# RetNet attention feeding a gated MLP on one core: the new state's product moved ahead of the state's product with the queries

## The chip, the cores and the metric

The kernel runs on one NeuronCore of a Trainium2 chip. The metric is the device time of one execution in microseconds (us), and the time of a kernel is the median over several executions.

## The reference

Two blocks stand one behind the other. The first is RetNet's parallel attention, with no softmax: for 8 batches, 8 heads, 576 positions and a head width of 64,

```python
scores = q @ k.T / sqrt(64)
gamma  = 1 - 2 ** (-5 - arange(8))                 # one decay for each head
Dmat   = where(i >= j, gamma ** (i - j), 0)        # i: query position, j: key position
ret    = (scores * Dmat) @ v
```

The heads' results are laid side by side as rows of `x`, 4608 tokens by 512. The second block is an MLP with a "serf" activation:

```python
h = x @ w_in                                       # 512 -> 2048
g = h * erf(softplus(h))
out = g @ w_out                                    # 2048 -> 512
```

All is in float32.

## The kernel before

**Attention in pieces.** The 4608 tokens are cut into 36 pieces of 128 tokens (`pieces`). Each pair of batches gives nine: four whole pieces of the first batch, four of the second, and a last one that holds the two batches' remaining 64 tokens each. Since the decay is a power, earlier tokens need not be multiplied again: their keys and values are summed into a *state* of 64 by 64 for each head, which is carried from piece to piece (`kept`). Decay factors are folded into the values (`gk`, on GpSimd in `weigh_values`), into the outputs (`gq`) and into the state (`gp`).

**Three stages for a piece.** `transposes` brings queries and keys to the layout that TensorE wants. For the first pieces TensorE does it (L332) with copies on ScalarE, for the later ones VectorE (L326), out of tiles `raw_qs` and `raw_ks` that SP's queue loads in 32-wide squares (L131). `scores` multiplies keys with queries (L347, 8 matmuls, tile `s`), and VectorE masks them into `sT` (L99). `outputs` is the stage that the change touches. It has up to three groups of 8 matmuls into two PSUM tiles of one bank each, `o[0]` and `o[1]`:

- the *outputs' products* (L365): values by masked scores, `o<-sT,raw_v`; contraction over 128 rows, 64 columns out, 128 moving columns
- the *state's products with the queries* (L376), `o<-qT,state`, only where the piece does not begin its batch: contraction over 64 rows, 64 columns out, 128 moving columns (64 in the nine-piece group's last piece, where two states are used)
- the *new state's product* (L388), `o<-raw_v,raw_k`, in whole pieces only: contraction over 128 rows, 64 columns out, 64 moving columns. It goes into the upper half of `o[0]`'s bank, which the code calls `kv`.

Of the 36 pieces, 8 begin a batch (no L376), 24 have all three groups, and 4 are the shared last ones (no L388).

VectorE then takes the results out, through the helper `tt` (L99): `scaled(1)` moves `o[1]`, times `gq`, into `x`; `sums` adds the old state to `kv`, and GpSimd multiplies by `gp` into `state` or `last` (L427; in a batch's first piece VectorE does that directly); `scaled(0)` moves `o[0]`. The four PSUM banks of the pool `ps_at` are shared in turn by `pt`, `s` and `o`.

**The MLP.** It works on chunks of 512 tokens and four slices of the hidden width. `First.product` (L496) is `x @ w_in`, `Second.product` (L604) is `g @ w_out`; both replace eight block products by seven with sums made on VectorE (a Strassen-Winograd form, `sums`, `operands_x`). In the first slice the first two chunks take a plain form (L550), and the last block of all has a form of its own (L668). Their matmuls are 128 by 128 with 256 moving columns. Weights are loaded in pieces and rounded by a chain of operations (`rounding`, L254 to L275) on ScalarE, VectorE and GpSimd.

**What sets the order.** The program's order is written by hand, and each engine works through its own instructions in that order. The stages stand in one list,

```python
    for i in range(len(pieces)):
        stages += [(transposes, i + 1), (outputs, i), (scores, i + 1)]
```

and `attend` issues the next one between steps of the MLP, so that a stage of attention alternates with a block product until the pieces are used up. A string at the start (`"alkakakawk..."`) orders the first chunk. SP's queue issues nearly all transfers in program order: `load(i + 2, "q")` at the end of `transposes(i)`, `load(i + 3, "kv")` at the end of `outputs(i)`, and stores of `x` and of partial outputs between them. Waits between engines are set by the framework from the tiles that instructions read and write.

Of the kernel before, what the change touches and what calls it, by code (L numbers as in the profile page):

```python
# [21 lines left out]
NP = H // 2  # L22
# [32 lines left out]
def kernel(  # L55
# [10 lines left out]
    nc = tc.nc  # L66
# [31 lines left out]
    def tt(out, in0, in1, op):  # L98
        nc.vector.tensor_tensor(out=out, in0=in0, in1=in1, op=op)  # L99

    def flat(ap):
        return ap.rearrange("p h d -> p (h d)")

    heads = [slice(e * D, (e + 1) * D) for e in range(2)]
# [45 lines left out]
    def load(i, names="qkv"):  # L150
        if i < len(pieces):
            t = loaded.setdefault(i, {})
            for name in names:
                src = {"q": q, "k": k, "v": v}[name]
                if name == "q" and i < SQUARES:
                    t["q"] = load_rows(i, "q", q, 2)
                elif name == "q":
                    t["qs"] = load_squares(i, "q", q)
                    if i >= SQUARES_K:
                        t["ks"] = load_squares(i, "k", k)  # L160
                elif name == "v" or i < SQUARES_K or len(pieces[i]) == 1:
                    t[name] = load_rows(i, name, src, 4)
# [137 lines left out]
    def x_tile():  # L300
        return xpool.tile([P, n_dc + 3, TCH], FP32, tag="x", name="x")
# [4 lines left out]
    def weigh_values(i):  # L306


        if i < len(pieces) and i not in weighed:
            weighed.add(i)  # L310
            t = (loaded.get(i) or live[i])["v"]
            by = gk if len(pieces[i]) == 1 else gk2
            nc.gpsimd.tensor_tensor(out=t, in0=t, in1=by.unsqueeze(2).to_broadcast([P, H, D]), op=ALU.mult)
# [40 lines left out]
    def outputs(i):  # L354
        segments = pieces[i]
        t = live.pop(i)
        seen = [(kept[b], r0, n) for b, s0, n, r0 in segments if s0 > 0]

        b, s0, n, _ = segments[0]
        o = [ps_at.tile([P, NP, P], FP32, tag="at", name=f"o{j}") for j in range(2)]
        for p in range(NP):
            for e in range(2):
                nc.tensor.matmul(  # L365
                    o[p % 2][heads[(e + p) % 2], p // 2, :],
                    lhsT=t["v"][:, 2 * p + e, :],
                    rhs=t["sT"][:, e, p, :],
                    start=(p < 2),
                    stop=(not seen and p >= NP - 2),  # L370
                    skip_group_check=True,
                )
        for state, r0, m in seen:
            for p in range(NP):
                for e in range(2):
                    nc.tensor.matmul(  # L376
                        o[p % 2][heads[(e + p) % 2], p // 2, r0 : r0 + m],
                        lhsT=state[heads[e], p, :],
                        rhs=t["qT"][heads[e], p, r0 : r0 + m],
                        start=False,  # L380
                        stop=(p >= NP - 2),
                        skip_group_check=True,
                    )
        if n == P:
            kv = flat(o[0])[:, 2 * P :].rearrange("p (a d) -> p a d", a=NP)
            for p in range(NP):
                for e in range(2):
                    nc.tensor.matmul(  # L388
                        kv[heads[e], p, :],
                        lhsT=t["k"][:, 2 * p + e, :],  # L390
                        rhs=t["v"][:, 2 * p + e, :],
                        start=False,
                        stop=(p == NP - 1),
                        skip_group_check=True,
                    )
        c, at = i // PC, i % PC * P
        if (0, c) not in x:
            x[0, c] = x_tile()

        def scaled(j):  # L400
            to = x[0, c][:, j:NP:2, at : at + P]
            if c < n_ch - 1:
                by = (gq if n == P else gq2)[:, j::2, :].unsqueeze(2).to_broadcast([P, 2, P // n, n])
                dst, got = (y.rearrange("p a (m i) -> p a m i", i=n) for y in (to, o[j][:, :2]))
                tt(dst, got, by, ALU.mult)
                return

            for r0 in range(0, P, n):
                dst = to[:, :, r0 : r0 + n].rearrange("p h (r a) -> p h a r", r=SQ)
                got, by = (  # L410
                    y.rearrange("p h (a r) -> p h a r", r=SQ)
                    for y in (o[j][:, :2, r0 : r0 + n], (gq if n == P else gq2)[:, j::2, :])
                )
                tt(dst, got, by, ALU.mult)

        scaled(1)
        if n == P:
            sums = kv
            if s0 > 0:
                sums = att.tile([P, NP, D], FP32, tag="sums", name="sums")  # L420
                tt(sums, kv, kept[b], ALU.add)

            if b % 2 == 0 and s0 + P + D == S:
                new = att.tile([P, NP, D], FP32, tag="last", name="last", bufs=1)
            else:
                new = att.tile([P, NP, D], FP32, tag="state", name="state")
            (nc.gpsimd if s0 > 0 else nc.vector).tensor_tensor(out=new, in0=sums, in1=gp, op=ALU.mult)  # L427
            kept[b] = new
        scaled(0)
        load(i + 3, "kv")  # L430
        if i + 1 >= SQUARES:
            weigh_values(i + 1)

    stages = [(transposes, 0), (scores, 0)]
    for i in range(len(pieces)):
        stages += [(transposes, i + 1), (outputs, i), (scores, i + 1)]
        if i in (PC + 1, 2 * PC - 1):
            stages[-3:-1] = stages[-2], stages[-3]
# [3 lines left out]
    def before_chunk(c):  # L442

        return stages.index((outputs, c * PC)) if c < n_ch else len(stages)

    def after_chunk(c):

        return stages.index((outputs, (c + 1) * PC - 1)) + 1
# [415 lines left out]
```

## Time and profile before

| | |
|---|---|
| median of 6 runs | 1027.73 us (1026.16 to 1028.47) |
| the profiled execution, device time | 1027.82 us |
| its span, first to last instruction | 1026.0 us |
| TensorE (PE) busy | 1018.2 us, 99% |
| VectorE (DVE) busy | 668.0 us, 65% |
| ScalarE (ACT) busy | 390.4 us, 38% |
| GpSimd (POOL) busy | 123.6 us, 12% |
| attention, first to last outputs' product | 11.0 to 315 us |
| granted TensorE clock | 1.00 |

In a row of the profile, "L376" is the line of the kernel, PE a matmul and PEld the load of its stationary operand, `o<-qT,state` the tile written and the tiles read. A form such as `64*64` names the part of the array that the instruction uses, rows by columns. A float32 matmul stands as two records, so a group of 8 shows as x16. In timelines the first column is the start in us, the second how long the row's instructions took together, and brackets hold idle time of the engine just ahead and what ended it.

### The profile page before, as it was taken

The numbers are of one execution on the slowest core, as the hardware profiler recorded it, in microseconds if no ns is written. First come the engines' busy times: TensorE is split into PE (matmuls) and PEld (weight loads), VectorE is DVE, ScalarE is ACT, GpSimd is POOL, SyncE is SP. The second block draws the span as 40 slices with busy tenths as digits, with TensorE's granted clock in tenths as the row PEclk, the third lists the DMA queues.
The fourth block names the chain that finished last, engine by engine and source line by source line (L and its number), as shares of the span: only waits on it lengthen the run. The fifth ranks groups of instructions, "written<-read, shape, count | busy, mean of one in ns | idle before, by whom it ended". The sixth has DMA issues, their size and how long they took to land.

```text
span 1026.0 us, 15958 instructions
## 1 busy us (share of the span) xinstructions
PE 1018.2 (99%) x6348; PEld 876.4 (85%) x6348; DVE 668.0 (65%) x1062; ACT 390.4 (38%) x481; POOL 123.6 (12%) x122
## 2 busy tenths in 40 slices
PE   9999999999999999999999999999999999999998
PEld 8787888888788888888888888888888888888887
DVE  3769777877876666656666666666567655555555
ACT  2354134233234444433443344444443333333332
POOL 2133122122311110010001001000100000000000
PEclk9999999999999999999999999999999999999999
DMA  9997989979984344544445344444433334444433
GB/s 198 201 246 166 235 190 228 251 152 247 233 180 168 129 144 144 167 162 160 154 147 174 123 144 154 167 152 144 144 124 124 123 128 128 131 135 131 127 88 118
DMA packets 146986, 165.76 MB, mean 162 GB/s; under 512 B 97376, under 2 KB 121568, under 8 KB 138848
## 3 DMA queue, kind: packets, MB, share of 16 engines
q1 hardware_dynamic: 144832, 163.57, 56.8%
q10 hardware_dynamic: 2080, 1.18, 0.5%
q8 instruction: 50, 0.82, 0.4%
q14 instruction: 24, 0.20, 0.1%
HBM read 117.52 MB, written 47.19 MB: 161 GB/s over the span
## 4 chain that ended last, share of the span: by engine, by line
PE 82%; DMA 10%; DVE 3%; SPq 3%; issue 1%; POOL 1%; ACT 0%; ACTq 0%; DVEq 0%; POOLq 0%
PE a L604 22%; PE a L496 21%; PE g L604 11%; PE g L496 11%; PE e L496 5%; PE e L604 5%; DMA raw_qs<-in_q_dram 4%; DMA raw_v<-in_v_dram 4%; PE o L365 2%; SPq L131 2%; PE s L347 2%; DMA raw_k<-in_k_dram 1%; SPq L147 1%; PE o L388 1%; PE o L376 1%
## 5 line engine op out<-in xcount | busy, mean ns | idle before, releaser
L496 PE MATMUL a<-x,wa 128*128 128x256 f32 x1088 | 258.3, 380 | 0.0
L496 PEld LDWEIGHTS a<-x,wa 128*128 128x128 f32 x1088 | 205.7, 190 | 28.5
L604 PE MATMUL a<-wb,s 128*128 128x256 f32 x840 | 200.0, 381 | 0.0
L604 PEld LDWEIGHTS a<-wb,s 128*128 128x128 f32 x840 | 158.4, 190 | 22.9 <-ACT o L618 0.7
L99 DVE TENSOR_TENSOR t<-g,t 128x512 f32<-128x512 f32 x68 | 46.9, 690 | 150.7 <-ACT t L526 113.1
L496 PE MATMUL g<-x,wa 128*128 128x256 f32 x544 | 129.2, 380 | 0.0
L496 PEld LDWEIGHTS g<-x,wa 128*128 128x128 f32 x544 | 102.8, 190 | 14.4
L99 DVE TENSOR_TENSOR o<-a,o 128x512 f32<-128x512 f32 x104 | 71.4, 686 | 46.5 <-PE a L604 46.5
L521 ACT COPY t<-a 128x512 f32<-128x512 f32 x34 | 19.9, 586 | 188.3 <-PE a L496 188.3
L99 DVE TENSOR_TENSOR t<-t,s 128x1024 f32<-128x1024 f32 x72 | 88.9, 1274 | 0.0
L565 ACT ACTIVATE s<-t 128x1024 f32<-128x1024 f32 x72 | 72.1, 1049 | 28.5 <-DVE t L99 28.4
L274 POOL TENSOR_TENSOR wraw<-wraw 128x512 f32<-128x512 f32 x28 | 29.5, 1052 | 438.4 <-DVE wraw L272 183.2
L99 DVE TENSOR_TENSOR x<-x 128x512 f32<-128x512 f32 x115 | 75.8, 692 | 1.2
L532 ACT COPY t<-a 128x512 f32<-128x512 f32 x34 | 19.9, 586 | 144.3 <-PE a L496 144.3
L569 ACT ACTIVATE s<-s 128x1024 f32<-128x1024 f32 x72 | 72.1, 1048 | 0.4
L604 PE MATMUL g<-wb,s 128*128 128x256 f32 x280 | 66.7, 381 | 0.3 <-DVE t L99 0.3
L604 PE MATMUL e<-wb,t 128*128 128x256 f32 x280 | 66.6, 380 | 0.0
L604 PE MATMUL a<-wb,t 128*128 128x256 f32 x280 | 66.6, 380 | 0.0
L604 PE MATMUL g<-wb,t 128*128 128x256 f32 x280 | 66.3, 380 | 0.0
L99 DVE TENSOR_TENSOR sT<-s,cst 128x512 f32<-128x512 f32 x72 | 46.1, 681 | 29.2 <-PE s L347 29.2
L496 PE MATMUL e<-x,wa 128*128 128x256 f32 x272 | 64.8, 381 | 0.0
L99 DVE TENSOR_TENSOR o<-g,o 128x512 f32<-128x512 f32 x70 | 47.9, 684 | 21.5 <-ACT o L618 18.8
(86 smaller groups left out, 1248.8 us busy)
## 6 DMA issues: line engine op xcount, KB each, us to landing
od<-o SPq DMA_DIRECT2D x54, 512.0 KB, 3.3
x<-xd SPq DMA_DIRECT2D x27, 1024.0 KB, 4.8
o<-od SPq DMA_DIRECT2D x27, 1024.0 KB, 5.1
raw_qs<-in_q_dram SPq DMA_DIRECT2D x96, 112.0 KB, 4.6
raw_ks<-in_k_dram SPq DMA_DIRECT2D x84, 112.0 KB, 4.2
xd<-x SPq DMA_DIRECT2D x9, 1024.0 KB, 5.2
raw_v<-in_v_dram SPq DMA_DIRECT2D x64, 128.0 KB, 4.6
wraw<-in_moe_w_in_dram SPq DMA_DIRECT2D x32, 256.0 KB, 5.9
```

Of the source, the lines that this page charges most:

```text
L99: nc.vector.tensor_tensor(out=out, in0=in0, in1=in1, op=op)
L131: nc.sync.dma_start(out=t[part * SQ : (part + 1) * SQ, :, at : at + m - SQ], in_=tokens[:, :, d0 : d0 + m - SQ])
L147: queue.dma_start(out=t[r0 : r0 + n, e::2, :], in_=heads.rearrange("h p d -> p h d"))
L274: engine.tensor_tensor(out=r_f, in0=high_f, in1=r_f, op=ALU.mult)
L347: nc.tensor.matmul(ps[e][:, p, :], lhsT=t["kT"][heads[e], p, :], rhs=t["qT"][heads[e], p, :], start=True, stop=True)
L365: nc.tensor.matmul(o[p % 2][heads[(e + p) % 2], p // 2, :], lhsT=t["v"][:, 2 * p + e, :], rhs=t["sT"][:, e, p, :], start=(p < 2), stop=(no ...
L496: nc.tensor.matmul(acc[:, j * TH : (j + 1) * TH], lhsT=weights["wa", self.g][:, a, d, j * P : (j + 1) * P], rhs=x[self.g, self.c][a][:, d, :],
L521: nc.scalar.copy(out=self.t1[:, 1], in_=self.a)
L532: nc.scalar.copy(out=self.t2[:, 0], in_=self.a)
L565: nc.scalar.activation(self.s[:, j], t, AF.Softplus)
L569: nc.scalar.activation(self.s[:, j], self.s[:, j], AF.Erf)
L604: nc.tensor.matmul(acc[:, tp, :], lhsT=left[:, j * TH + tp * P : j * TH + (tp + 1) * P], rhs=weights["wb", self.g][:, b, j, :], start=(sta ...
```

## The change

The new state's product stands directly behind the outputs' products, and the state's products with the queries come last. On VectorE, `sums` (or the state itself, in a batch's first piece) is issued ahead of `scaled(1)`, which now directly precedes `scaled(0)`. Nothing is added or removed; in the built program ACT's and SP's instructions stand in the same order as before, and POOL's too.

```diff
-        for state, r0, m in seen:
-            for p in range(NP):
-                for e in range(2):
-                    nc.tensor.matmul(
-                        o[p % 2][heads[(e + p) % 2], p // 2, r0 : r0 + m],
-                        lhsT=state[heads[e], p, :],
-                        rhs=t["qT"][heads[e], p, r0 : r0 + m],
-                        start=False,
-                        stop=(p >= NP - 2),
-                        skip_group_check=True,
-                    )
         if n == P:
             kv = flat(o[0])[:, 2 * P :].rearrange("p (a d) -> p a d", a=NP)
             for p in range(NP):
...
+        for state, r0, m in seen:
+            for p in range(NP):
+                for e in range(2):
+                    nc.tensor.matmul(
+                        o[p % 2][heads[(e + p) % 2], p // 2, r0 : r0 + m],
+                        lhsT=state[heads[e], p, :],
+                        rhs=t["qT"][heads[e], p, r0 : r0 + m],
+                        start=False,
+                        stop=(p >= NP - 2),
+                        skip_group_check=True,
+                    )
         c, at = i // PC, i % PC * P
...
-        scaled(1)
         if n == P:
             sums = kv
...
             (nc.gpsimd if s0 > 0 else nc.vector).tensor_tensor(out=new, in0=sums, in1=gp, op=ALU.mult)
             kept[b] = new
+        scaled(1)
         scaled(0)
```

## The prediction

> **What bounds the kernel now.** I read the page first, for who is busy:
>
> ```profile
> span 1026.0 us, 15958 instructions
> PE 1018.2 (99%) x6348; PEld 876.4 (85%) x6348; DVE 668.0 (65%) x1062; ACT 390.4 (38%) x481; POOL 123.6 (12%) x122
> ...
> PEclk9999999999999999999999999999999999999999
> DMA  9997989979984344544445344444433334444433
> ```
>
> PE has no hole to speak of at full clock, and the DMA engines are near full for the first third, while attention runs (to 315 us), and half idle after it. So time comes off only where PE issues less, or waits less. Next the list of PE's waits, to see what there is to lose or win:
>
> ```profile
> PE pt_q L332 <- DMA raw_q<-in_q_dram: 0.7, 1, 0.7
> PE s L347 <- DVE kT L326: 0.7, 1, 0.7
> PE pt_k L332 <- DMA raw_k<-in_k_dram: 0.4, 1, 0.4
> PE s L347 <- DVE qT L326: 0.4, 1, 0.4
> PE g L604 <- DVE t L99: 0.3, 1, 0.3
> ```
>
> No matmul of the changed stage is in it, and in the same list for the loads only the outputs' products wait for a mask (`sT`, 1.3 us in 4 waits): PE never waits for `state`. An earlier state is thus worth nothing by itself. What can matter is the order on PE, so I read the timeline of one stage with all three groups (106 us) and one that begins a batch (115 us):
>
> ```profile
> 106.12 0.85 PEld L365 LDWEIGHTS o<-sT,raw_v 128*64 128x64 f32 x16 [0.33 <-issue]
> ...
> 107.15 0.43 PEld L376 LDWEIGHTS o<-qT,state 64*64 64x64 f32 x16 [0.17 <-issue]
> ...
> 107.75 0.55 PEld L388 LDWEIGHTS o<-raw_v,raw_k 128*64 128x64 f32 x16 [0.17 <-issue]
> ...
> 108.36 1.59 PEld L604 LDWEIGHTS g<-wb,t 128*128 128x128 f32 x8
> ...
> 115.03 0.85 PEld L365 LDWEIGHTS o<-sT,raw_v 128*64 128x64 f32 x16 [0.33 <-issue]
> ...
> 115.84 0.60 PEld L388 LDWEIGHTS o<-raw_v,raw_k 128*64 128x64 f32 x16
> 116.52 0.51 PEld L496 LDWEIGHTS a<-x,wa 128*128 128x128 f32 x3
> ```
>
> Wherever the form changes (128\*64, 64\*64, 128\*128), the loads pause. Where outputs are followed by the new state's product, both 128\*64, there is no pause. That order occurs 8 times already, and the change makes it the rule. Last the chain of waits, for what could take a gain back:
>
> ```profile
> 37.06 0.42 DVE state L427
> ...
> 42.58 1.09 PE o L365 x14
> ...
> 249.56 6.07 DMA wraw<-in_moe_w_out_dram
> ...
> 260.75 4.75 DMA raw_qs<-in_q_dram
> ...
> 272.64 1.16 PE s L347 x16
> ```
>
> From 158 to 272 us this chain holds transfers, SP and DVE but no PE: PE reaches 272 us only 0.7 us too early. A faster PE will find these loads in its way.
>
> **The change on PE.** Times between the starts of successive groups' loads, in ns. Before, in a stage with all three: outputs 1024, state 598, new state 615, together 2237 (equal within 1 ns in 19 of the 24; the other five contain waits). In the 8 batch beginnings: outputs 819, new state 670, together 1489. After the change a stage is that 1489 plus a state group. Its 598 was measured from a change of form to the next, which is what it has again: the last moving width sets the pause (172 ns behind a width of 128, 68 behind 64, each over two different pairs of forms). So 1489 + 598 = 2087, and 2237 − 2087 = 0.150 us a stage, 24 × 0.150 = 3.6 us if all is kept. If instead the pause belonged to the pair of forms, the new state would take 774 and the state 498: 819 + 774 + 498 = 2091, or 3.5 us. Nothing hangs on that. Bounds on the two boundaries not seen (new state to state; a state of width 128 to the MLP): the nearest rows are those, so I take 0.15 with both ends near.
>
> A rule speaks against this: the Trainium skill, "TensorE: Matmul & The Clock Gate", Part 3, says that a load overlaps running matmuls only if they use other rows of the array. Outputs and new state both use all 128 rows, so by it the boundary would cost its 205 ns again and the whole gain would be near nothing. The trace shows otherwise: at 115.84 us the loads run on, 35 ns ahead of the end of the last output's load. I go with the trace. The other rule, in "TensorEngine Tiling (Array Packing)", Tiling Modes, is that a change of mode drains the array; one of three changes goes, and with the 175 ns of drain on the first page (Single matmul latency) that is an estimate of 4.2 us. The row's 0.150 is net of the longer first group behind it and is used.
>
> **The change on the other engines.** DVE: the same three operations in another order. `sums` does not get free behind the new state's product: it reads `o[0]`, and in the built program it waits for the sixth of the eight state products, the last one into that tile. At the stage of 97 us PE's last product ended at 99.60, DVE began `x` at 98.98, `sums` at 99.64, `x` at 99.97, and was free for the next at 100.30. After: the stage ends 0.15 earlier, the sixth product 0.11 before that (two of eight in 0.43), so `sums` at 99.31, `x` at 99.64 and 99.97, free at 100.30. No change on DVE; the `sums` wait holds up only these two. In a batch's first piece `scaled(1)` used to run beside the new state's product and now stands behind the state operation: DVE is free 0.33 later (starts of 37.06 and 37.40) if it had been waiting there. It was in 3 of 8 (12.1, 36.6, 116.2 us). Of these 36.6 is on the chain, as DVE then works without a gap to the mask that outputs wait for at 42.58: +0.3 us there. The one at 116 is covered: masks end 2.1 us ahead of the outputs around it.
>
> POOL: `state` at most 0.2 us earlier; nobody waits for it. ACT, SP: same order; SP's loads of k and v wait for buffers that come free up to 0.6 us earlier. The new state's product is read for 0.6 us earlier, which needs `raw_k` that was issued three stages before.
>
> **What is kept.** PE's gain lasts until the next moment that others set. Stage by stage:
> - 16, 20, 25 us: lost, since PE then waits for raw_q at 33.9 us.
> - 42, 53, 58 us: +0.45, less 0.3 from DVE, but at 81.8 and 88.3 us PE waits for DVE (0.4 and 0.1), whose chain goes back to weight rounding and loads: about 0.
> - 87.8 to 211.9 us, 11 stages: 1.65. PE waits nowhere, and SP issues each piece's queries when DVE has freed their buffer, so loads follow PE to about 222 us.
> - 220.8, 249.6, 258.8, 267.7 us: up to 0.6, lost in the waits at 252 and 272 us, if transfers stay where they are.
> - 289, 298, 307 us: 0.45, kept; behind them PE alone runs to the end.
>
> Together 2.1 us, with perhaps 0.1 of the doubtful ones: 2.2. The profiled execution took 1027.82 (span 1026.0 and 1.8 around it), within 0.1 of the median, so both give 1025.5.
>
> **The rivals.**
> *All is kept* (chance 0.22): loads move with PE throughout. For it: PE's waits after 36 us are 1.6 us in all, and 1027.8 − 1.6 = 1026.2 is the fastest run, so waits differ from run to run. 1027.7 − 3.6 = 1024.1.
> *Transfers take more* (0.20): if the chain without PE from 158 to 272 us is rigid, only six stages before it (0.9) and three behind it (0.45) count, less DVE's 0.3: 1.0, so 1026.7. For it: DMA busy at 0.9 and more. Against it: SP's waits for DVE all along that stretch.
> *DVE becomes the bound, slower* (0.07): it gains nothing in the 24 stages and loses 0.33 in each batch beginning, where `scaled(1)` leaves the shadow of the new state's product. If masks had no lead, PE's 3.6 would turn into waiting, and 8 × 0.33 = 2.6 us be added: 1030.3. It decides once the mask's lead over the outputs is under 0.33 us. Against it: the lead is 2.3 us in most stages, and DVE waits for PE in 3 of the 8 only.
> *It does not do what it says*: the state is hardly earlier, by the wait above. That is certain, and costs nothing.
>
> **How the numbers follow.** Likeliest, at 0.51: 1025.5, alone within 1024.7 to 1026.3. A measurement of this kernel can tell about 0.2%, 2.06 us, so this case lies on the edge; I give it 0.30 to faster and 0.21 to no difference. All kept: 0.22 to faster. Transfers: 0.20 to no difference. DVE: 0.07 to slower. Sum: 0.52, 0.41, 0.07. The range takes in all kept less 0.2 for scatter, 1023.9, and the transfers' case plus 0.6 for it, 1027.3.
>
> **What would show it.** Right: loads of the new state's product (L377 in the changed kernel, L388 being the state's) start some 0.82 us behind those of L365 with no pause in all 32 stages, and stages with three groups take 2.09 us. The waits for kT or t near 252 and 272 us grow by about 0.5 us. Wrong: a pause ahead of L377; a state group over 0.65 us; new PE waits for `sT` in many stages; the last outputs' product earlier than 314.0 us by under 1 or over 3 us.

## The result, and the profile after

The changed kernel takes 1026.06 us (median of 34 runs, 1024.10 to 1027.59) against 1027.28 us before (68 runs): the ratio is 0.9986, 95% interval 0.9982 to 0.9991, or 1.4 us less (0.9 to 1.9). The interval leaves out 1, so the gain is real, though smaller than the 0.2% that the prediction took as the least that one measurement of this kernel can tell. The profiled execution took 1024.89 us (span 1023.1), among the quickest of its 34. A second trace of the same kernel, of an execution of 1026.17 us (span 1024.4), is read beside it. The trace of before is of an execution of 1027.82 us, 0.5 us above the median, so what separates two traces is not the gain by medians.

From the page after:

```profile
span 1023.1 us, 15955 instructions
PE 1014.3 (99%) x6348; PEld 876.6 (86%) x6348; DVE 667.4 (65%) x1062; ACT 390.4 (38%) x481; POOL 122.6 (12%) x122
...
DMA  9997989979974344544444345444433334444433
...
PE 87%; DMA 4%; DVE 3%; SPq 3%; issue 1%; ACT 1%; POOL 1%; ACTq 0%; DVEq 0%; POOLq 0%
```

PE's busy time fell from 1018.2 to 1014.3 us, 3.9 us; the span of this execution fell by 2.9 us, that of the second trace by 1.6 us. So the stage did shrink, and part of it came back as idle time. The timeline of the two stages shown before (start in us, then how long the row took):

```profile
105.20 0.85 PEld L365 LDWEIGHTS o<-sT,raw_v 128*64 128x64 f32 x16 [0.33 <-issue]
...
106.02 0.60 PEld L377 LDWEIGHTS o<-raw_v,raw_k 128*64 128x64 f32 x16
...
106.69 0.42 PEld L388 LDWEIGHTS o<-qT,state 64*64 64x64 f32 x16
...
107.29 1.38 PEld L604 LDWEIGHTS g<-wb,t 128*128 128x128 f32 x7 [0.17 <-issue]
```

```profile
113.96 0.85 PEld L365 LDWEIGHTS o<-sT,raw_v 128*64 128x64 f32 x16 [0.33 <-issue]
...
114.78 0.60 PEld L377 LDWEIGHTS o<-raw_v,raw_k 128*64 128x64 f32 x16
```

L377 is now the new state's product and L388 the state's with the queries. From the start of the outputs' loads to those of the new state it is 0.82 us with no pause, then 0.67, then 0.60 to the MLP: 2.09 us for what took 2.24. A stage that begins a batch is as before. The waits of PE in the same trace (who waited for whom: us in total, times, longest):

```profile
PE pt_q L332 <- DVE x L99: 1.0, 1, 1.0
PE s L347 <- DVE kT L326: 0.8, 2, 0.6
...
PE g L604 <- DVE t L99: 0.5, 1, 0.5
PE o L365 <- issue: 0.4, 1, 0.4
```

and in the second trace:

```profile
PE s L347 <- DVE kT L326: 1.3, 2, 1.0
...
PE g L604 <- DVE t L99: 0.6, 1, 0.6
```

Between 88 us and PE's last product the waits for `kT` and `t` are the only ones listed: 1.3 and 1.9 us in sum where it was 1.0 before (at 252 and 273 us), now near 231, 250 and 271 us. Where the lead over the kernel before grows and where it goes is seen when the starts of the outputs' products are subtracted stage by stage (us; worked out from the traces, the first column being the time in the trace of before):

| stage at | changed kernel | second trace | fewer issues on SP (below) |
|---|---|---|---|
| 87.8 | 0.62 | 1.00 | 0.64 |
| 220.8 | 2.28 | 2.67 | 2.31 |
| 238.0 | 1.76 | 2.42 | 2.46 |
| 267.7 | 1.85 | 2.14 | 3.10 |
| 277.4 | 2.47 | 1.36 | 3.99 |
| 314.0 | 2.92 | 1.81 | 4.44 |

From 88 to 221 us the lead grows by 1.65 in each, which is eleven stages of 0.15. From 221 to 277 us, with four more stages that have all three groups, it should grow by another 0.6; instead it moves by +0.2 in one trace and −1.3 in the other. The chain of waits shows that this piece of the run is the one PE does not govern (start, length):

```profile
204.43 1.92 PE a L496 x8
219.56 5.16 DMA wraw<-in_moe_w_in_dram
224.74 5.38 DMA raw_ks<-in_k_dram
...
247.90 6.42 DMA wraw<-in_moe_w_out_dram
254.33 3.85 DMA raw_ks<-in_k_dram
...
270.17 1.16 PE s L347 x16
```

PE is on it up to about 212 us (before: 158) and again from 270 us. Twice in these rows a load of `raw_ks` starts 0.01 to 0.02 us behind the end of a weights' transfer (219.56 + 5.16 = 224.72, and 247.90 + 6.42 = 254.32): its issue waited for that transfer to land, that is, to be complete. What remains to be found is what holds the loads back between 212 and 270 us.

### The profile page after: what moved, and what is told of

Its sections match the earlier page's. It is cut to its first block, busy times and chain, and to the rows that moved or that the text cites. A ratio compares the mean times of both kernels' runs of the same rounds, so it can differ in the third digit from the quotient of the medians.

```text
span 1023.1 us, 15955 instructions
## 1 busy us (share of the span) xinstructions
PE 1014.3 (99%) x6348; PEld 876.6 (86%) x6348; DVE 667.4 (65%) x1062; ACT 390.4 (38%) x481; POOL 122.6 (12%) x122
## 4 chain that ended last, share of the span: by engine, by line
PE 87%; DMA 4%; DVE 3%; SPq 3%; issue 1%; ACT 1%; POOL 1%; ACTq 0%; DVEq 0%; POOLq 0%
PE a L604 23%; PE a L496 22%; PE g L496 11%; PE g L604 11%; PE e L604 6%; PE e L496 5%; PE o L365 2%; PE s L347 2%; SPq L147 2%; DMA wraw<-in_moe_w_in_dram 2%; PE o L388 1%; PE o L377 1%; DMA raw_ks<-in_k_dram 1%; PE f L668 1%; DMA wraw<-in_moe_w_out_dram 1%
```

## The experiments

**One engine's order at a time.** The change reorders two engines. The first kernel takes PE's new order with VectorE's old one, the second the reverse. Against the changed kernel the first reads

```diff
+        scaled(1)
         if n == P:
             sums = kv
...
-        scaled(1)
         scaled(0)
```

> The change's order on TensorE alone; VectorE keeps its order of before (scaled(1), then sums, then scaled(0)). Loss on other waits alone (my theory: TensorE saves 24 x 0.15 = 3.6 us and some 2.2 of it come back as waits for loads and for VectorE's weight chain): as the changed kernel within 0.4 us, so about 1.2 to 1.4 us under before. Rival, that VectorE's new order ate the rest: 0.3 us or more faster than the changed kernel, up to 3 us under before. In the trace stages with three groups take 2.09 us as in the changed kernel.

> VectorE's new order alone (sums or the state operation ahead of scaled(1)); TensorE keeps the order of before. My theory: TensorE saves nothing, stages with three groups 2.24 us; VectorE is 0.33 us later at most where it had been waiting in the piece that begins a batch: between 0 and 0.4 us slower than before, not to be told from it. Rival, that VectorE's order is what ate the gain: slower than before by 1.5 to 2.5 us.

Measured: 1026.68 us, ratio 0.9987 (0.9979 to 0.9995), and 1027.50 us, ratio 0.9999 (0.9990 to 1.0007). PE's order alone gives what the whole change gives, and VectorE's order alone gives nothing. In the trace of the first the lead is 1.90 us at the stage of 212 us and 0.39 at that of 277 us. So VectorE's order is not what eats the gain.

**Leaving loads out.** Both kernels with the squares of queries and keys loaded once and used again, from piece 8 (queries) and 12 (keys) on; later pieces thus compute with the queries and keys of that one load. The work of PE, VectorE, ScalarE and GpSimd stays, and SP has 12 issues of squares in place of 236 (the 180 of the expectation below are those of whole pieces).

```diff
+    once = {}
     def load_squares(i, name, src):
-        t = raw.tile([P, NP, P * D // SQ], FP32, tag=name + "s", name=f"raw_{name}s", bufs=2)
+        if name in once:
+            return once[name]
+        t = once[name] = cpool.tile([P, NP, P * D // SQ], FP32, name=f"once_{name}s")
```

> Before, with the loads of queries and keys in squares made once and used for all later pieces (L131 issues 12 transfers in all instead of 180): the attention of pieces 8 on is computed from the wrong queries and keys, all instructions on the engines stay. It shows what before waits for those loads. My theory: TensorE's waits at 252 and 272 us go, 0.5 to 1.5 us under before.

> The changed kernel with the same loads left out (queries and keys of pieces 8 on are wrong). My theory: against the other kernel without these loads it keeps the 18 late stages in full, 18 x 0.15 = 2.7 us, and up to 0.9 of the early ones: 2.7 to 3.4 us faster than it, twice what the change brings with the loads in place. Rival, that the loss is on VectorE or in the early stages: the difference stays at 1.2 to 1.5 us.

Measured: the order of before 1026.72 us (ratio to before 0.9991, 0.9983 to 0.9999), the new order 1023.59 us (0.9962, 0.9949 to 0.9974). With the loads out of the way the change is worth 3.1 us of the 3.6 that 24 stages of 0.15 make, and neither trace has a PE wait between 88 us and PE's last product. So what is missing with the loads in place, about 1.7 us, is given back to these loads. That leaves open whether SP issues them too slowly, the DMA engines move them too slowly, or an issue has to wait for earlier transfers, as all were relieved.

**Another order, and the change once more.** If a stage starts with the state's products, which need no mask, PE may find work where it waits for masks at 42 and 88 us; the number of changes of form is the same as in the changed kernel. Against the kernel before, the loop over `seen` moves up and takes over the start of the sum in PSUM, and the outputs' products keep its end; VectorE's order stays. The changed kernel was measured again beside it.

```diff
+        for s, (state, r0, m) in enumerate(seen):
...
+                        start=(s == 0 and p < 2),
+                        stop=False,
...
         for p in range(NP):
             for e in range(2):
...
-                    start=(p < 2),
-                    stop=(not seen and p >= NP - 2),
+                    start=(not seen and p < 2),
+                    stop=(p >= NP - 2),
...
-        for state, r0, m in seen:
```

> The changed kernel once more, so that it stands on the same chip as the next three: 1.0 to 1.6 us under before.

> Before, with the state's products with the queries moved the other way: ahead of the outputs' products (they take start=True where there are any), the new state's product behind the outputs, VectorE's order as before. Forms change just as often as in the changed kernel (64*64, 128*64, then the MLP). My theory that a pause belongs to a change of form: TensorE's stage 598 + 819 + 670 = 2087 ns, the same 3.6 us less; since scaled(1) is again in the shadow of the new state's product, and TensorE does the state's products while it waits for the masks (0.4 us at 42 us, 0.1 at 88), 0 to 0.8 us faster than the changed kernel, the rest still lost to the loads at 230 to 272 us. Rival, that only the boundary between outputs and new state counts for its own sake: the same. Rival, that the state comes too late for this place: new TensorE waits for POOL state, slower than the changed kernel.

> The same, with the square loads of queries and keys made once (pieces 8 on are computed from wrong queries and keys): as the changed kernel without these loads (1023.6 us) or up to 0.8 us faster, and 3.0 to 4.0 us under the kernel before without them.

Measured: the change again 1026.17 us (0.9988, 0.9981 to 0.9994); state first 1024.12 us (0.9967, 0.9955 to 0.9980); state first with the squares' loads left out as above 1021.90 us (0.9947, 0.9933 to 0.9960). In its timeline the state's products start at 104.09 us, the outputs' at 104.69, the new state's at 105.51 and the MLP at 106.18: 0.60, 0.82 and 0.67 again make 2.09 us. What it has over the change comes early: its lead over the kernel before is 1.88 us at the stage of 97 us (1.48 in the trace of its second run, below), where the change has 0.77 (1.16 in the second trace), and the wait of the outputs at 42 us is not in its list. The leads at one moment scatter, but not what a stage adds: from 78 to 97 us both traces of this order gain 0.85 to 0.88 us, and both of the change 0.32 to 0.33. Later it waits for `kT` and `t` as the change does (1.9 us between 230 and 270 us, 2.5 in its second run).

**Moving loads to another queue.** The rows of k and v from piece 9 on, issued by ScalarE's queue:

```diff
-                queue = nc.scalar if (name, i) == ("k", 0) else nc.sync
+                queue = nc.scalar if (name, i) == ("k", 0) or i > SQUARES else nc.sync
```

> The changed kernel, with the rows of keys and values of pieces 9 on issued by ScalarE's queue in place of SP's: as many bytes and packets, a third fewer issues on SP (about 0.5 us each, 4 of some 14 a piece). If SP's time to issue is what makes the loads late at 230 to 272 us: those waits shrink, 0.5 to 1.2 us faster than the changed kernel. If the transfers' own rate is (DMA share at or over 1.0 there): as the changed kernel within 0.4 us, or slower where ScalarE's copies now stand behind an issue that waits for a buffer.

Measured: 1056.25 us, ratio 1.0284 (1.0268 to 1.0300). PE waits for the same thing, only far more, and SP for rows that ScalarE's queue now issues (second fence):

```profile
PE s L347 <- DVE kT L326: 19.3, 6, 6.5
```

```profile
SPq L131 <- DMA raw_k<-in_k_dram: 75.2, 28, 7.7
```

In the changed kernel SP's loads of squares wait 0.3 us for `raw_k`. The traces show how a load can wait for another load: the transfers of both queues use eight semaphores in turn, and in none of 702 cases here, nor of as many in the changed kernel and in the kernel before, does a transfer start before the one ahead of it on its semaphore has landed (worked out from the traces). So at most eight transfers are under way, and where ScalarE's queue issues one of them, SP's queue waits for that landing. Between 88 and 330 us SP's pauses that end with the landing on the semaphore come to 132 us here, to 18 in the changed kernel. A miss for the theory of SP's issues: SP has fewer of them, and the loads come later. Beside the issues' time and the DMA engines' rate there is thus a third candidate, the wait for earlier landings.

**More issues, the same bytes.** In the changed kernel each load of v's rows, from piece 9 on, is split in two. State first was measured a second time beside it.

```diff
-                queue.dma_start(out=t[r0 : r0 + n, e::2, :], in_=heads.rearrange("h p d -> p h d"))
+                rows = heads.rearrange("h p d -> p h d")
+                if name == "v" and i > SQUARES:
+                    queue.dma_start(out=t[r0 : r0 + n, e : H // 2 : 2, :], in_=rows[:, : NP // 2])
+                    queue.dma_start(out=t[r0 : r0 + n, H // 2 + e :: 2, :], in_=rows[:, NP // 2 :])
```

> The changed kernel with each load of v's rows, from piece 9 on, issued as two of half the heads: the same bytes and the same 256-byte rows, but 2 more issues on SP's queue per whole piece (4 in the shared last ones), some 27 pieces, at about 0.5 us an issue as SP's rows show. Theory that SP's issue time makes the loads late near 230 to 272 us: about 1 us more per piece on SP, of which what piles up between 212 and 272 us (six pieces) shows as PE waits, so several us slower than the changed kernel, 1028 to 1033. Rival, that the DMA engines' rate does: within 0.5 us of the changed kernel, 1025.6 to 1026.7, with the waits near 231, 250 and 271 us as they were (sum about 2 us).

> The kernel with the state's products first in the stage, then the outputs' products, then the new state's product, again in a run of its own. If its lead over the changed kernel is real: 1023.3 to 1024.9, ratio to before 0.9955 to 0.998. If it was scatter of one job: 1025.5 to 1026.5, as the changed kernel.

Measured: 1036.62 us, ratio 1.0082 (1.0068 to 1.0095), and for state first 1025.22 us, 0.9968 (0.9956 to 0.9980), the same lead as in its first run. With more issues PE's waits after 88 us are (L352 is the scores' line here, L370 the outputs'):

```profile
PE s L352 <- DVE kT L331: 6.4, 2, 3.8
PE o L370 <- POOL raw_v L318: 1.5, 1, 1.5
```

7.9 us in place of 1.3. The time is above the expected window, by clock that the longer waits cost (last section). SP's own timeline ahead of the largest of them, up to 240.91 us, where the two half pieces of a shared piece are loaded, and the DMA engines meanwhile (second fence: window, PE busy, and towards the end the granted clock, the DMA share and GB/s):

```profile
225.39 0.61 SPq L150 DMA_DIRECT2D raw_v<-in_v_dram  x1
...
228.99 0.61 SPq L150 DMA_DIRECT2D raw_v<-in_v_dram  x1
229.64 1.25 SPq L242 DMA_DIRECT2D wraw<-in_moe_w_in_dram  x2
```

```profile
225.00:230.00 5.00, 5.00 (x73) 4.15 (x70) 4.97 (x12) 0.44 (x1) 0.61 (x1) 1.00 0.20 45
```

From 213 to 235 us SP makes no pause longer than 0.11 us (two of its issues take 1.3 and 1.6 us, for a reason that the trace does not show), while the DMA engines are at 0.20 from 225 to 230: they have little to do because SP has not yet got to the loads of queries and keys. Here neither the rate of the DMA engines nor a landing makes these loads late, but the issuing; only the last issue of `raw_ks`, at 235.47 us, comes 1.1 us later for a landing. The wait of 2.6 us up to 197.65 is of another kind: the last three issues of `raw_ks` ahead of it, at 189.91, 190.95 and 191.93 us, each start 0.01 to 0.02 us behind the landing of a weights' transfer eight issues before. So more issues alone can make the loads late, and waits for landings can as well.

**Fewer issues, the same bytes.** The mirror of it: v's rows (from piece 9) and k's (from piece 12) with one issue for all eight heads. The heads then lie in another order in the tile, so the matmuls pick them by `head`, and GpSimd weighs the values in that order.

```diff
+    def whole(i, name):
+        return name == "v" and i > SQUARES or name == "k" and i >= SQUARES_K
+    def head(i, name, p, e):
+        return e * NP + p if whole(i, name) else 2 * p + e
...
         for b, s0, n, r0 in pieces[i]:
+            if whole(i, name):
+                nc.sync.dma_start(out=t[r0 : r0 + n], in_=src[b, :, s0 : s0 + n, :].rearrange("h p d -> p h d"))
+                continue
             for e in range(2):
```

> The changed kernel with the rows of v (from piece 9 on) and of k (from piece 12 on) loaded by one issue for all eight heads in place of two for four heads each: the same bytes and 256-byte rows, two issues less on SP's queue per piece, about 1 us per piece. GpSimd's weighing of the values walks the heads in another order there. Theory that SP's issue time makes the loads late: the waits near 231, 250 and 271 us (1.3 to 2.3 us in sum in the changed kernel) vanish or nearly so, 1023.6 to 1024.6, close to the run without the squares' loads. Rival, that the DMA engines' rate or the landing time of the transfers does: waits as they were, 1025.7 to 1026.5.

> The same loads in the kernel with the state's products first in the stage. By the theory of SP's issue time its waits of 1.9 to 2.5 us near 231, 250 and 270 us vanish: 1021.7 to 1023.2, near the run of this order without the squares' loads. By the rival: 1024 to 1025.3, as without the edit.

Measured: in the changed kernel 1025.19 us, ratio 0.9969 (0.9958 to 0.9981); with state first 1022.94 us, 0.9959 (0.9944 to 0.9973). On this chip the kernel before took 1028.36, so the absolute time of the first is above the expected window by 0.6, while its distance to before, 3.2 us, is what the theory asked for; its interval just parts from that of the change alone (0.9982 to 0.9991). The trace has no PE wait from 88 us to PE's last product. The stretch in the changed kernel, and then with fewer issues (columns as above):

```profile
220.00:240.00 20.00, 19.40 (x192) 15.79 (x192) 16.86 (x30) 3.16 (x6) 5.20 (x5) 1.00 0.96 230
...
260.00:280.00 20.00, 19.80 (x185) 16.27 (x184) 19.97 (x33) 3.33 (x6) 8.10 (x7) 1.00 1.06 258
```

```profile
220.00:240.00 20.00, 20.00 (x202) 16.34 (x200) 17.73 (x31) 3.49 (x6) 5.79 (x6) 1.00 1.06 236
...
260.00:280.00 20.00, 20.00 (x186) 16.73 (x187) 19.72 (x33) 3.50 (x6) 8.10 (x7) 1.00 1.12 253
```

PE goes from 19.40 and 19.80 (19.52 between them) to 20.00 throughout, while the DMA engines are no less busy: they could carry more, so their rate was not the bound. What SP's queue gained shows in its own waits between 216 and 272 us (summed from the lists of waits): for other engines, whose buffers it needs, 12.4 us here against 4.9 and 1.7 in the two traces of the changed kernel; for landings 5.7 against 6.7 and 9.9. SP's queue is what makes the loads late, and most of the room that it won is time of issues. But a transfer of eight heads also moves more with each of the eight semaphores, so this edit does not part the issues' time from the landings. State first with fewer issues has one PE wait left, of 0.2 us at 268 us, and has the lowest median of the kernels that do all the work, 5.4 us under the one before by medians and 4.2 us by the ratio (2.8 to 5.8), though its interval overlaps with that of state first alone.

## Why the prediction was right or wrong

The prediction was 1025.5 us in a range that holds the measured 1026.06. The gain that it forecast, 2.2 us, is above the measured 1.4 (0.9 to 1.9); the time comes closer than the gain in part because the prediction counted from 1027.73, 0.45 us above the later median of before. By its steps:

- *0.150 us a stage, 24 times 3.6 us.* Right within 2 ns: stages with three groups take 2.085 to 2.086 us where nothing disturbs them (19 of 24), against 2.087 predicted, and there is no pause ahead of L377 in any of them. The two boundaries that could not be seen ahead came out as taken, with pauses of 68 ns from new state to state and 172 ns from the state to the MLP. The rule of the Trainium skill ("TensorE: Matmul & The Clock Gate", Part 3) that a load overlaps only with matmuls on other rows was rightly set aside: the loads of L377 run behind those of L365 as they did before in stages that begin a batch. The same part also lets a load go ahead that targets a background weight buffer, which the prediction left out; the trace does not show which buffer a load goes to.
- *VectorE, +0.33 us where it waits in a batch's first piece.* Right in size and place. At the stage of 36 us VectorE came free 0.17 us earlier although PE was 0.50 earlier, and the wait of the outputs at 42 us grew from 0.07 to 0.41 us. VectorE's order alone has that wait too and costs nothing that can be measured.
- *`sums` starts ahead of the stage's end.* Not seen: at 98.71 us it starts 0.10 behind the end of the state's products, not 0.1 ahead of it, and VectorE waits there in 8 of 24 stages. In this one it costs VectorE 0.16 us (its next operation starts 0.61 us earlier than before, PE's stage 0.77), but no time of the kernel, by the first pair of experiments.
- *16 to 58 us: about nothing.* The lead at 88 us is 0.62 and 1.00 us in the two traces. But the kernel before with the loads left out, whose order on PE is unchanged, also leads by 0.56 there, so this says how loads fall in the first 90 us more than what the change does. A wait of 1.0 us at 25 us, of PE for VectorE, was not foreseen and is lost in the same place.
- *87.8 to 211.9 us: 1.65 us; 289 to 307 us: 0.45 us.* Right: 1.65 and 1.66, 0.45 and 0.45 in the two traces.
- *220.8 to 267.7 us: up to 0.6, lost in the waits at 252 and 272 us.* Here the sum failed. It let these waits take back at most what those four stages bring. They can take earlier gain too: from 221 to 277 us the lead changed by +0.2, −1.3 and, with PE's order alone, −1.3 us, where the sum has +0.1. The waits at 252 and 272 us, which were to grow by about 0.5, went from 0.27 and 0.67 us to 0.48 and 0.20 in the first trace and to 0.63 and 1.02 in the second, and a wait at 231 us (0.60 and 0.33) is new. The early 0.6 to 1.0 us that the sum put at about nothing have the other sign, so that the two errors partly cancel in the traces: that the time lies so near the likeliest case is in part luck.

The step behind it is the sentence that SP issues each piece's queries when VectorE has freed their buffer, so that loads follow PE to about 222 us. They follow as long as SP waits for VectorE. From 216 us on SP seldom does; in the changed kernel it reads

```profile
220.26 1.97 SPq L131 DMA_DIRECT2D raw_qs<-in_q_dram  x4
222.32 3.11 SPq L131 DMA_DIRECT2D raw_ks<-in_k_dram  x4
226.65 0.98 SPq L147 DMA_DIRECT2D raw_k<-in_k_dram  x2
227.74 0.99 SPq L147 DMA_DIRECT2D raw_v<-in_v_dram  x2
228.83 2.18 SPq L131 DMA_DIRECT2D raw_qs<-in_q_dram  x4
```

and so on. A piece costs SP about 6 us of issues (the first four rows add to 7.05 us, of which 1.08 is a pause inside the second), and the weights' loads and the stores come on top. Of the 56 us from 216 to 272 us, 44 are issues, some of them drawn out by a wait inside, and 7.2 are pauses that end with a landing, among them those 1.08 us and the 1.2 us ahead of `raw_k` at 226.65 (41 and 11.0 us in the second trace). An earlier PE hurries neither, and the prediction's sum counts neither. The rival in which transfers take more (1026.7) had the stretch right and the cause in part: it is SP's queue, with its issues and its waits for landings, and not the rate of the DMA engines, which is why the loss can be had back without moving fewer bytes. It also began too early, at 158 us. VectorE as the bound, the slower rival, did not show: the first pair of experiments finds no cost of its new order.

Open: how the waits at 231 to 271 us fall differs from run to run (1.3 and 1.9 us in two traces of one kernel), and what decides it is not known. No run parts the time of SP's issues from its waits for landings as the cause of them. And the 29 us that the same rows cost on ScalarE's queue are traced to SP's waits for landings, but not divided up.

## What to carry to other kernels

Group matmuls by the part of the array that they use: here one change of form fewer was worth 0.15 us per stage, and it can be read from the old trace wherever the wanted order already occurs once. Put the group whose operands have long been ready first in its stage, so that it fills waits of the others. And before counting a gain of the busiest engine as kept, read the timeline of the queue that issues its loads: where its issues and its waits for landings leave no room, gain can be lost there. In this kernel fewer and larger transfers gave it back, and a second queue did not.

## What the runs showed of the hardware

An issue's price on SP depends little on what it carries. Between 88 and 330 us the median issue of v's rows took 0.47 us for two heads (106 issues, the kernel with more of them), 0.51 for four (52, the changed kernel) and 0.61 for all eight (26, the kernel with fewer), worked out from the traces. Four times the bytes cost 1.3 times as much, which is one reason why merging pays.

The pause between two groups of different form goes with the width of the first one's matmuls as long as the loads are alike. Behind loads of 64 columns it is 172 ns for 128 moving columns and 68 for 64, in both kernels. Behind the scores' products, which also have 128 moving columns, it is 121 ns; but their loads have 128 columns and take 188 ns in place of 137, so that from the start of the last load to the start of the next group it is 309 ns in both cases.

And a long pause of PE costs twice. In the kernel with more issues PE waited 2.6 us up to 197.65 and 3.8 us up to 240.91, and the granted clock (last column but two) then fell to half, in the first case for some 7 us:

```profile
197.00:199.00 2.00, 1.35 (x12) 1.35 (x14) 2.00 (x6) 0.00 (x0) 0.58 (x1) 0.58 1.08 394
...
201.00:203.00 2.00, 2.00 (x6) 1.55 (x6) 0.64 (x2) 0.00 (x0) 0.00 (x0) 0.50 1.11 208
```

Time times missing clock is 3.4 us here and 1.7 us behind the second pause. With the 6.6 us of added waits that is 11.7 of the 12.0 us by which this span exceeds that of the changed kernel. The pause of 1.5 us up to 322.88 had no such sequel. In the kernel whose rows ScalarE's queue issues, one of 2.0 us up to 66.17 did (0.50 from 68 to 70 us), and one of 1.7 us up to 131.48 did not. The Trainium skill, "TensorE: Matmul & The Clock Gate", Part 1, has PE at half clock after an idle window of about 3.4 us; the second pause agrees with that; the first one, of 2.6 us, and the one of 2.0 us are shorter than the page asks for.
